# Attention and routed experts on one core: two banks for the turned weights, and a new order inside a step

## The chip, the cores and the metric

The kernel runs on one core of a Trainium2 chip. The metric is device time in microseconds, the median of several executions. Before the change it is 627.34 us (three executions, 626.08 to 628.61).

## The reference

The program computes attention with a window of 32 positions (heads 0 to 3) or with a window of 128 of which every fourth counts (heads 4 to 7), and sends the result, token by token, through one of eight experts. Cut to what matters:

```
B, H, S, D = 8, 8, 576, 64
scores = q @ k.T / sqrt(D), masked per head (rel < 32, or rel < 128 and rel % 4 == 0)
attn   = softmax(scores);  x = (attn @ v), laid out as (4608, 512)
logits = x @ w_gate                      # (4608, 8)
e      = argmax(logits, axis=1);  gate = softmax(logits)[e]
out    = gate * (relu(x @ w1[e]) @ w2[e])   # w1: 8 x 512 x 1024, w2: 8 x 1024 x 512
```

## The kernel before

The attention is worked off in 36 blocks of 128 rows, nine for each of the four batch pairs. One call of `step(n)` works on several blocks at once: it makes the scores of block n, turns the weights of block n - 1, multiplies by the values for block n - 2, turns the finished rows of block n - 3 and makes the routing logits of block n - 4. Steps 0 to 34 (`MEND = 35`) stand in a section in which TensorE, VectorE, ScalarE and SyncE issue strictly in the order in which the code names their work; the steps after that are put in order by the scheduler. After the attention come the experts, with TensorE busy nearly throughout.

The stages that the change touches, with their lines:

- `st_scores` (L290): 32 products of 64 x 64 tiles into the tiles `s` (one bank for each half g of the heads), after `st_mask` (L274) has written the mask there, one step earlier. A half's bank is free when `st_sub` has read it.
- `st_max` (L301) and `st_sub` (L306), VectorE: the maximum of a half, and the scores less the maximum into `d`. `d` is one tile for both halves and has one buffer.
- `st_exp` (L316), ScalarE: the exponential from `d` into `p`. `p` is one tile for both halves and has one buffer too.
- `st_trans` (L322), TensorE: four transposes of one half of `p` into the PSUM tile `pt`, tag `T`, one bank. `st_ptcopy` (L327), ScalarE: copies `pt` into `pts` (two buffers), and with that frees the bank.
- `st_av` (L337), TensorE: 32 products of `pts` with the values into `o` (one buffer of two banks). VectorE reads `o` in `st_z` (L347), `st_rz` (L352) and `st_x` (L357), which makes the rows `xs` and frees `o`.
- `st_xt` (L389), TensorE: four transposes of the rows into `tp`; `st_xcopy` (L397), ScalarE, copies them out.
- `st_logits` (L405), TensorE, in every third step (6, 9, 12 and so on): eight products into `ps_l`, tag `L`, one bank. `st_keep` (L418, L428), ScalarE, copies them out at the end of the step.
- Routing: after every ninth block `turn` (L485) transposes logits, first six tiles and one step later three. Groups 0 and 2 go to the bank with tag `E`, group 1 goes to tag `L`. VectorE reads them (L490). Other routing work of VectorE is drawn from a list by `pull_off` and `pull_spaced`, at fixed places of the step.
- `first.turn_x`, `first.high_x`, `first.low_x` (L806, L809, L813): in the two steps 35 and 36 the rows of the first expert's tokens are transposed and split into a high and a low part.
- In steps 9 to 13 ScalarE also makes the high halves of early expert weights (`high`, L742), at the end of a step.

PSUM has eight banks here: `X` one, `S0` and `S1` one each, `T` one, `O` two, `L` one, `E` one.

Of the kernel before, what the change touches and what calls it, by code (L numbers as in the profile page):

```python
# [9 lines left out]
F32 = mybir.dt.float32  # L10
# [17 lines left out]
P = 128  # L28
# [3 lines left out]
HP = H // 2  # L32
# [127 lines left out]
def attention_moe_kernel(ctx, tc, qk, v, wg, w, cst, tok, end, slots, mask, zero, out):  # L160
# [32 lines left out]
    psa = att.enter_context(tc.tile_pool(name="psa", bufs=1, space=PSUM))  # L193
# [17 lines left out]
    def load_qk(n):  # L211
        if n < total:
            nc.sync.dma_start(qkr[:, n % NRQ], qk[n])

    def load_v(n):
        if n < total:
            nc.sync.dma_start(vr[:, n % NRV], v[n])
# [98 lines left out]
        nc.scalar.activation(st["p", n][:, g], st["d", n][:, g], AF.Exp, scale=0.125)  # L316

    def st_trans(n, g):
        pt = psa.tile([P, HP, P], F32, tag="T", name="pt")
        st["pt", n] = pt  # L320
        for h in range(HP):
            nc.tensor.transpose(pt[:KB, h], st["p", n][:, g, h], ident)  # L322
# [69 lines left out]
    NG = 3  # L392
# [6 lines left out]
    def st_logits(n):  # L399
        if n % NG < NG - 1:  # L400
            return
        xt = st.pop(("xt", n // NG))
        ps_l = psa.tile([P, NG, P], F32, tag="L", name="ps_l")
        for c in range(4):
            nc.tensor.matmul(  # L405
                ps_l[32 * c : 32 * (c + 1)], lhsT=wgz[:, c], rhs=xt[:, c], start=True, stop=True
            )
        st["l", n] = ps_l
# [43 lines left out]
    def pull_pe(late=False):  # L452
        if side and side[0][0] == (2 if late else 1) and (
            ticks[0] - ticks[1] >= GAP or now[0] >= FREE
        ):
            side.pop(0)[1]()

    def pull_spaced():
        if slow:
            slow.pop(0)()  # L460

    def pull_off():
        ticks[0] += 1
        if side and not side[0][0]:
            ticks[1] = ticks[0]
            side.pop(0)[1]()

    def route(m, then=None, after=None):
# [7 lines left out]
        def turn(k):  # L476
            for k in k:
                if k % 2:
                    tl = psa.tile([P, NG, P], F32, tag="L", name="tl")
                else:  # L480
                    tl = pse.tile([P, NG, P], F32, tag="E", name="tl")
                    taken[0] = True
                for i in range(NG):
                    t = NG * k + i
                    nc.tensor.transpose(tl[:, i], lgs[:, t * P : (t + 1) * P], ident)  # L485
                box["tl", k] = tl
# [78 lines left out]
        def enter(ts):  # L565
# [3 lines left out]
            for t in ts:  # L569
                s1, b1 = hot.pop(t)  # L570
                nc.tensor.matmul(box["tb"], lhsT=s1, rhs=b1, start=t == 0, stop=t == NT - 1)

        on_pe(turn, (0, 1), late=True)
        off_pe(gather_parts, 0)
        off_pe(gather_parts, 1)
        on_pe(turn, (2,), late=True)
        off_pe(gather_parts, 2)
        off_both(
# [498 lines left out]
    first = statics[0]  # L1077
# [52 lines left out]
    def go(f, n):  # L1130
        if 0 <= n < total:
            f(n)

    def both(f, n, g):
        if 0 <= n < total:
            f(n, g)

    def step(n):
        now[0] = n
        if not turning or taken[0]:  # L1140
            pull_pe(late=True)
        go(st_scores, n)
        load_qk(n + 5)
        load_v(n + 3)
        turned = turning.pop(0) if turning and not taken[0] else None
        if turned is not None:
            first.turn_x(turned)
        both(st_trans, n - 1, 0)
        both(st_ptcopy, n - 1, 0)
        if turned is not None:  # L1150
            first.high_x(turned)
        both(st_max, n, 0)
        both(st_sub, n, 0)
        pull_spaced()
        go(st_av, n - 2)
        both(st_trans, n - 1, 1)
        both(st_ptcopy, n - 1, 1)
        both(st_exp, n, 0)
        both(st_max, n, 1)
        both(st_sub, n, 1)  # L1160
        go(st_xt, n - 3)
        go(st_xcopy, n - 3)
        both(st_exp, n, 1)
        if turned is not None:
            first.low_x(turned)
        else:
            pull_off()
        go(st_z, n - 2)
        go(st_rz, n - 2)
        pull_off()  # L1170
        go(st_x, n - 2)
        pull_spaced()
        go(st_xout, n - 2)
        pull_off()
        go(st_logits, n - 4)
        go(st_keep, n - 4)
        pull_pe(late=True)
        go(st_mask, n + 1)
        for _ in range(2):
            if spare:  # L1180
                high, low = spare.pop(0)
                high()
                low()
        pull_off()
        pull_pe()
        pull_off()
        for f in todo.pop(n, []):
            f()

    with tc.manual_schedule(engines=ENGS | {mybir.EngineType.SP}):  # L1190
        st_mask(0)
        for n in range(MEND):
            step(n)
    n = MEND
    while n < total + 5 or todo or spare:
        step(n)
        n += 1
# [367 lines left out]
```

## Time and profile before

| | |
|---|---|
| median of three executions | 627.34 us |
| the profiled execution, its own time | 627.71 us |
| its span, first to last instruction | 625.9 us |
[...]
| TensorE products busy | 601.3 us, 96% |
| VectorE busy, ScalarE busy | 340.5 us, 313.2 us |
| scores of step 3 to scores of step 35 start | 18.29 to 154.13 us |

In the rows below a line of the timeline gives start in us, duration in us, engine, line of the code, operation, tile written and tiles read, and how many instructions were merged. What stands in brackets is idle time of the engine just before, and who ended it. PE is the product, PEld the loading of its weights, DVE is VectorE, ACT is ScalarE, SPq is the queue of SyncE.

### The profile page before, as it was taken

The page shows a single profiled execution, that of the slowest core. Times are in us where ns is not written, and L with a number is a line of the kernel's source. Part 1 is how long each engine was busy: PE and PEld are TensorE (multiplying, and loading weights), DVE is VectorE, ACT ScalarE, POOL GpSimd, SP SyncE. Part 2 cuts the span into 40 slices and gives each one's busy share as a digit, 9 for nine tenths or more (in the row PEclk, how much of TensorE's full clock was granted, in tenths as well). Part 3 has the DMA queues.
Part 4 walks back from the last instruction along what each step waited for, and adds up shares of the span by engine and source line. Part 5 has one row for each costly group of instructions (what it writes and reads, how often), then busy time and mean ns, then how long its engine had stood idle before and what let it go on. Part 6 is the DMA issues. An engine that isn't in the chain of part 4 may idle for free. (4 is left out here: it accounts for less than half of the span.)

```text
span 625.9 us, 13313 instructions
## 1 busy us (share of the span) xinstructions
PE 601.3 (96%) x5299; PEld 490.4 (78%) x5299; DVE 340.5 (54%) x754; ACT 313.2 (50%) x606; POOL 249.3 (40%) x296
## 2 busy tenths in 40 slices
PE   7999999999989999999999999999999999999992
PEld 6877787788878888788888888888888888888771
DVE  3876787888593544563457255625643573453000
ACT  2668766676533541563456256535644563552110
POOL 0336666476826620451245125312522341253520
PEclk8999999999999999999999999999999999999997
DMA  8999999994237650573476267717743763476710
GB/s 319 411 384 414 413 403 410 396 331 139 66 99 230 208 185 29 181 257 117 151 241 231 84 221 240 241 55 236 259 162 112 243 234 119 172 241 252 276 49 21
DMA packets 43359, 138.17 MB, mean 221 GB/s; under 512 B 9008, under 2 KB 10416, under 8 KB 43248
## 3 DMA queue, kind: packets, MB, share of 16 engines
q1 hardware_dynamic: 23088, 78.30, 34.5%
q0 software_dynamic: 19776, 58.52, 27.0%
q8 instruction: 42, 0.69, 0.4%
q10 hardware_dynamic: 432, 0.49, 0.2%
q14 instruction: 21, 0.17, 0.1%
HBM read 117.65 MB, written 21.63 MB: 223 GB/s over the span
## 5 line engine op out<-in xcount | busy, mean ns | idle before, releaser
L731 DVE TENSOR_TENSOR wu<-raw,wu 128x512 fp32r<-128x512 f32 x200 | 128.7, 687 | 103.7 <-ACT wu L730 103.7
L877 PE MATMUL yps<-wu,h 128*128 128x512 f32 x696 | 170.5, 396 | 0.4 <-DVE wu L731 0.4
L846 PE MATMUL hps<-x,wu 128*128 128x512 f32 (+1 forms) x720 | 164.0, 385 | 0.2 <-DVE h L858 0.2
L846 PEld LDWEIGHTS hps<-x,wu 128*128 128x128 f32 x720 | 132.0, 188 | 27.6 <-DVE h L858 0.7
L877 PEld LDWEIGHTS yps<-wu,h 128*128 128x128 f32 x696 | 128.0, 188 | 27.4 <-DVE wu L731 0.8
L730 ACT CAST wu<-raw 128x512 fp32r<-128x512 f32 x200 | 113.3, 621 | 27.8 <-DMA raw<-in_w_dram,wi 17.2
L922 POOL DMA_INDIRECT raw<-in_w_dram,wi x40 | 39.4, 985 | 98.3 <-DVE wu L731 90.7
L858 DVE SCALAR_TENSOR_TENSOR h<-hps,h 128x512 fp32r<-128x512 f32 (+1 forms) x60 | 40.1, 670 | 47.8 <-ACT h L857 47.6
L327 ACT COPY pts<-pt 96x512 f32<-96x512 f32 x72 | 41.9, 582 | 46.7 <-PE pt L322 45.9
L767 POOL DMA_INDIRECT out_dram<-y,both_i x30 | 32.7, 1091 | 80.2 <-ACT y L766 60.1
L857 ACT ACTIVATE h<-hps 128x512 fp32r<-128x512 f32 (+1 forms) x60 | 34.8, 581 | 59.4 <-PE hps L846 52.3
L766 ACT ACTIVATE y<-yps,both_i 128x512 f32<-128x512 f32 x28 | 19.3, 688 | 68.5 <-PE yps L877 36.1
L301 DVE TENSOR_REDUCE nm<-s 128x4 f32<-128x384 f32 x72 | 39.5, 550 | 25.0 <-PE s L290 24.5
L322 PE MATMUL pt<-ident,p 128*96 128x128 f32 x288 | 47.3, 288 | 3.2 <-ACT pts L327 2.8
L337 PE MATMUL o<-vr,pts 96*64 96x65 f32 x1152 | 43.7, 227 | 2.0 <-issue 1.9
L337 PEld LDWEIGHTS o<-vr,pts 96*64 96x64 f32 x1152 | 38.1, 139 | 9.4 <-issue 8.4
L369 POOL DMA_DIRECT2D x_d<-xs x36 | 20.6, 572 | 60.9 <-DVE xs L357 26.3
L756 POOL DMA_INDIRECT xg<-x_d,both_i x30 | 32.2, 1074 | 29.5 <-PE tpx L806 11.5
L306 DVE TENSOR_TENSOR d<-s,nm 128x384 f32<-128x384 f32 x72 | 40.1, 557 | 4.6
L316 ACT ACTIVATE p<-d 128x384 f32<-128x384 f32 x72 | 37.6, 524 | 6.6 <-DVE d L306 6.6
L973 PE MATMUL ypd<-wu,hd 128*128 128x512 f32 x168 | 40.4, 391 | 0.0
L941 PE MATMUL hpd<-wu,xd 128*128 128x512 f32 x168 | 40.2, 393 | 0.0
(169 smaller groups left out, 680.7 us busy)
## 6 DMA issues: line engine op xcount, KB each, us to landing
raw<-in_w_dram SPq DMA_DIRECT2D x64, 512.0 KB, 4.3
qkr<-in_qk_dram SPq DMA_DIRECT2D x36, 576.0 KB, 8.3
vr<-in_v_dram SPq DMA_DIRECT2D x36, 520.0 KB, 8.8
x_d<-xs POOLq DMA_DIRECT2D x44, 128.0 KB
t_in<-tab SPq DMA_DIRECT2D x3, 320.0 KB
x_d<-xs POOLq DMA_DIRECT2D x8, 112.0 KB
x_d<-xs POOLq DMA_DIRECT2D x8, 96.0 KB
tab<-in_zero_dram SPq DMA_DIRECT2D x2, 320.0 KB
```

What stands on the lines that cost most here:

```text
L301: nc.vector.tensor_reduce(st["nm", n][:, g], st["s", n][g], axis=AX.X, op=ALU.max)
L306: nc.vector.tensor_tensor(st["d", n][:, g], st["s", n][g], st["nm", n][:, g].broadcast_to([P, HP, KB]), op=ALU.subtract,)
L322: nc.tensor.transpose(pt[:KB, h], st["p", n][:, g, h], ident)
L327: nc.scalar.copy(st["pts", n][:, g], st.pop(("pt", n))[:KB])
L337: nc.tensor.matmul(st["o", n][QB * j : QB * (j + 1), g, h], lhsT=pts[:, g, h, QB * j : QB * (j + 1)], rhs=vr[:KB, n % NRV, a : a + DH + 1] ...
L730: nc.scalar.copy(u[:, 0, sl], raw[:, sl])
L731: nc.vector.tensor_tensor(u[:, 1, sl], raw[:, sl], u[:, 0, sl].bitcast(F32), op=ALU.subtract)
L846: nc.tensor.matmul(hps[:, : self.ns], lhsT=u[:, wpart, fs], rhs=self.x[:, xpart, c, : self.ns], start=(k == 0), stop=(k == 11),)
L858: nc.vector.scalar_tensor_tensor(h[:, 1, :n], hps[:, :n], 0.0, h[:, 0, :n].bitcast(F32), op0=ALU.max, op1=ALU.subtract,)
L877: nc.tensor.matmul(yps, lhsT=self.h[f][:, hpart, ts], rhs=u[:, wpart, fs], start=f == 0 and k == 0, stop=f == 7 and k == 2,)
L941: nc.tensor.matmul(hps, lhsT=self.x[:, xpart, c], rhs=u[:, wpart, ns], start=(k == 0), stop=(k == 11),)
L973: nc.tensor.matmul(self.yps, lhsT=self.h[f // 4][:, hpart, f % 4], rhs=u[:, wpart, fs], start=f == 0 and k == 0, stop=f == 7 and k == 2,)
```

## The change

The tile `pt` gets two banks (tag `T`, `bufs=2`). The bank with tag `L` goes: the logits `ps_l` and the routing's group 1 (`tl`) are now taken from the same two banks `T`. The count of banks stays eight. Inside the step the order becomes: scores of block n, maximum and difference of its first half, values of block n - 2, the first expert's transposes where there are any, both halves of the turned weights of block n - 1, rows of block n - 3. The first exponential of block n is named between the first half's transposes and its copy, so on ScalarE it stands ahead of both copies of block n - 1, where it stood behind both. `first.high_x` moves from behind the first copy to behind the rows' transposes.

```
     def st_trans(n, g):
-        pt = psa.tile([P, HP, P], F32, tag="T", name="pt")
+        pt = psa.tile([P, HP, P], F32, tag="T", bufs=2, name="pt")
...
-        ps_l = psa.tile([P, NG, P], F32, tag="L", name="ps_l")
+        ps_l = psa.tile([P, NG, P], F32, tag="T", bufs=2, name="ps_l")
...
-                    tl = psa.tile([P, NG, P], F32, tag="L", name="tl")
+                    tl = psa.tile([P, NG, P], F32, tag="T", bufs=2, name="tl")
...
         turned = turning.pop(0) if turning and not taken[0] else None
+        both(st_max, n, 0)
+        both(st_sub, n, 0)
+        go(st_av, n - 2)
         if turned is not None:
             first.turn_x(turned)
         both(st_trans, n - 1, 0)
+        both(st_exp, n, 0)
         both(st_ptcopy, n - 1, 0)
-        if turned is not None:
-            first.high_x(turned)
-        both(st_max, n, 0)
-        both(st_sub, n, 0)
-        pull_spaced()
-        go(st_av, n - 2)
         both(st_trans, n - 1, 1)
         both(st_ptcopy, n - 1, 1)
-        both(st_exp, n, 0)
+        pull_spaced()
         both(st_max, n, 1)
         both(st_sub, n, 1)
         go(st_xt, n - 3)
+        if turned is not None:
+            first.high_x(turned)
         go(st_xcopy, n - 3)
         both(st_exp, n, 1)
```

## Rows read from the trace of the kernel before

**Rows 1.** The page, busy time, share and instructions of each engine.

```profile
PE 601.3 (96%) x5299; PEld 490.4 (78%) x5299; DVE 340.5 (54%) x754; ACT 313.2 (50%) x606; POOL 249.3 (40%) x296
```

**Rows 2.** Waits from 0 to 175 us: us in total, times, longest.

```profile
ACT pts L327 <- PE pt L322: 45.9, 48, 2.6
...
PEld pt L322 <- ACT pts L327: 4.7, 10, 1.3
...
PE pt L322 <- ACT pts L327: 2.8, 6, 1.2
```

**Rows 3.** Timeline of TensorE, step 8, to the scores of step 9.

```profile
37.77 0.83 PE L290 MATMUL s<-qkr 64*64 64x96 f32 x32
38.53 0.64 PE L322 MATMUL pt<-ident,p 128*96 128x128 f32 x4
39.10 1.15 PE L337 MATMUL o<-vr,pts 96*64 96x65 f32 x32
40.19 0.64 PE L322 MATMUL pt<-ident,p 128*96 128x128 f32 x4
40.66 0.60 PE L389 MATMUL tp<-ident,xs 128*128 128x128 f32 x4
41.20 0.36 PE L274 MATMUL s<-mk 64*64 64x384 bf16 x4
41.38 0.83 PE L290 MATMUL s<-qkr 64*64 64x96 f32 x32
```

**Rows 4.** Timeline of ScalarE, from the second copy of step 8 on.

```profile
40.87 0.58 ACT L327 COPY pts<-pt 96x512 f32<-96x512 f32 x1 [1.07 <-PE pt L322]
41.35 0.52 ACT L316 ACTIVATE p<-d 128x384 f32<-128x384 f32 x1
41.77 0.57 ACT L397 COPY xt<-tp 128x512 f32<-128x512 f32 x1
42.24 0.53 ACT L316 ACTIVATE p<-d 128x384 f32<-128x384 f32 x1
```

**Rows 5.** Timeline of VectorE, step 8, then the second half of step 17.

```profile
38.66 0.56 DVE L301 TENSOR_REDUCE nm<-s 128x4 f32<-128x384 f32 x1 [0.37 <-PE s L290]
39.33 0.56 DVE L306 TENSOR_TENSOR d<-s,nm 128x384 f32<-128x384 f32 x1
...
40.38 0.56 DVE L306 TENSOR_TENSOR d<-s,nm 128x384 f32<-128x384 f32 x1
...
41.28 0.69 DVE L357 TENSOR_TENSOR xs<-o,rz 128x512 f32<-128x512 f32 x1
...
81.62 0.56 DVE L306 TENSOR_TENSOR d<-s,nm 128x384 f32<-128x384 f32 x1
...
82.87 0.69 DVE L357 TENSOR_TENSOR xs<-o,rz 128x512 f32<-128x512 f32 x1
```

**Rows 6.** Timeline of TensorE, end of step 6: rows, logits, next mask.

```profile
32.59 0.60 PE L389 MATMUL tp<-ident,xs 128*128 128x128 f32 x4
33.12 0.85 PE L405 MATMUL ps_l<-xt,wgz 128*32 128x384 f32 x8
33.90 0.36 PE L274 MATMUL s<-mk 64*64 64x384 bf16 x4
```

**Rows 7.** Timeline, step 13: first copy, second turned half, routing's transposes.

```profile
63.13 0.58 ACT L327 COPY pts<-pt 96x512 f32<-96x512 f32 x1
...
63.77 0.64 PE L322 MATMUL pt<-ident,p 128*96 128x128 f32 x4 [1.17 <-ACT pts L327]
...
64.68 0.82 PE L485 MATMUL tl<-ident,lgs 128*128 128x128 f32 x6
```

**Rows 8.** Line 306 by itself: separate wait instructions in VectorE's queue, ns min/median/max.

```profile
L306 DVEq EVENT_SEMAPHORE  x32: 21/21/21, 11.0 to 156.7; - x32
```

**Rows 9.** Busy time from 160 to 200 us: length, then each engine.

```profile
160.00:200.00 40.00, 38.05 (x287) 31.18 (x282) 23.80 (x76) 16.50 (x36) 21.61 (x25) 1.00 0.44 136
```

**Rows 10.** Waits of SyncE's queue for TensorE, the values' loads.

```profile
SPq L217 <- PE o L337: 21.3, 16, 3.2
```

## The prediction

> **What bounds the kernel now.** I read the page first: TensorE's products are busy 96% of the span, VectorE 54%, ScalarE 50% [rows 1]. So whatever lengthens TensorE's sequence lengthens the kernel, and nothing else does until it makes TensorE wait. Then I read the waits of the attention: the one that the first edit aims at is TensorE waiting for the copy of turned weights, 2.8 us of idle products and 4.7 us of idle weight loads [rows 2]; the 45.9 us that ScalarE waits for TensorE are no loss by themselves. Then the timeline of one plain step, step 8. The reader should see that TensorE has no hole in it: scores to turned half 0.76 us, to values 0.57, to turned half 1.09, to rows 0.47, to the next mask 0.54, to the next scores 0.18, together 3.61 us [rows 3]. VectorE ends its second difference at 40.94, and the mask that needs it comes at 41.20 [rows 3, 5]; ScalarE idles 1.07 us ahead of the second copy [rows 4]. Both have a little air, and the question is whether the new order keeps it.
>
> In what follows S is the start of a step's scores and a the start of its values. A step ends when the mask for the next can be written.
>
> **TensorE's own sequence.** The new order is scores, values, half, half, rows, mask. Values to half 1.09, half to half 0.47 (as half to rows today), rows 0.47, mask 0.54, scores 0.18 are all in [rows 3]; only scores to values is new. Scores to a half takes 0.76 and cannot be less, since the 32 products themselves fill it. Going into the values costs 0.57 where a half to the rows costs 0.47, so 0.10 more for the entry. I take 0.76 + 0.10 = 0.86, since the values are entered here too: the plain step is then 0.86 + 1.09 + 0.47 + 0.47 + 0.54 + 0.18 = 3.61 us, unchanged. The bounds are 0.76 (no entry cost) and 0.95 (leaving the tiles of the scores costs as much again): over the 33 steps with values -3.3 to +3.0 us.
>
> [...]
>
> **The exponential ahead of the copies.** On ScalarE the order was copy, copy, exponential; it becomes exponential, copy, copy. `p` has one buffer, and the first exponential of block n writes the tile that both halves of block n - 1 are turned from. Does it wait for one half or for both? `d` is built alike, and there the trace tells: the first difference starts 0.67 us after its maximum, the separate wait instructions are 32 for 72 differences [rows 5, 8], so about one for each step and not one for each half. I take it that the buffer is given back whole. Then the second half, begun at a + 1.09 + 0.47, is with ScalarE 0.68 us later (40.19 to 40.87 [rows 3, 4]), and the exponential starts at a + 2.24. An exponential to the next instruction takes 0.42, a copy to the next 0.48 [rows 4]: the first copy starts at a + 2.66 and ends at a + 3.24, and TensorE sees it 0.06 later (63.13 + 0.58 to 63.77 [rows 7]), at a + 3.30. The second is done at a + 3.14 + 0.64 = a + 3.78. The next values come at a + 3.61 and need its half only after 16 of their 32 products, so they don't wait.
>
> **Logits without a bank of their own.** In every third step TensorE comes to the logits at a + 1.09 + 0.47 + 0.47 + 0.53 = a + 2.56 [rows 3, 6]. Both `T` banks then hold turned weights, and the first is free at a + 3.30. That is 0.74 us of waiting, with the mask and the next scores queued behind it on TensorE. Steps 6 to 36 have eleven logits that meet turned weights: +8.1 us. `st_keep` frees its bank well before the next step's second half, so it adds nothing.
>
> **The routing's group 1.** It comes 0.91 us after the second half's start plus half of the six transposes, 0.41 [rows 7], so at a + 1.56 + 0.91 + 0.41 = a + 2.88, and waits 0.42 for the same copy. Three routings in the ordered steps: +1.3 us.
>
> **The second exponential.** It starts after both copies and the rows' copy (0.48, 0.48, 0.47 [rows 4]) at a + 4.09 and is done at a + 4.68, which is S + 5.54, or 1.93 into the next step if this one was plain. There the first difference wants to start at 39.33 - 37.77 = 1.56 [rows 3, 5] and must wait for `d`: 0.37 late. The second difference then ends at 2.61 + 0.37 + 0.56, the mask may start 0.06 later, at 3.60, and TensorE comes to it at 3.43: a wait of 0.17 in a plain step that follows a plain one. After logits or routing the longer step hides it. Some five such steps are left: +0.9 us.
>
> **VectorE's rows.** The values now want `o` at S + 0.86, where they wanted it at S + 1.33. The rows of step 8 start at 41.28 and end at 41.97, 0.59 into the next step, so by themselves they pass. Where routing work stands before them (1.25 us after the second difference in step 17, against 0.90 [rows 5]) and the difference is late too, they miss by some tenths: 0 to 1 us in all, I take 0.5.
>
> **What the second bank gives.** The waits for the copy go, those of step 13 above all (1.17 us behind ScalarE's weight work [rows 7]): between 2.8 and 4.7 us [rows 2], I take 3.7.
>
> **Other moves, costed at nothing.** `pull_spaced` keeps its place on VectorE. The values free their slot earlier, so SyncE's loads, which wait 21.3 us for that [rows 10], go out up to half a microsecond earlier; no value load bounds a step. POOL's stores follow the rows, with slack as now. `high_x` comes behind both copies in steps 35 and 36, which makes the low part, and the bank `E` behind it, later: 0 to 2 us. After 160 us TensorE is idle 1.95 us of 40 [rows 9], and at most that much of a delay could vanish there. I set these two against each other.
>
> **Sum:** 8.1 + 1.3 + 0.9 + 0.5 - 3.7 = +7.1 us. The profiled execution, 627.71 us by itself (span 625.9), stands 0.37 above the median of 627.34, so the forecast is 634.5 us. About 0.5%, 3.1 us, is what a measurement of this kernel can tell from no change: 624.2 to 630.5.
>
> **The rivals.** (1) Not slower: halves are given back one by one. Then the exponential starts after the first half, at a + 1.09 + 0.68 = 1.77, the first copy is seen at a + 2.83, the logits wait 0.27 (3.0 us in all), group 1 not at all, and the second exponential is 0.47 earlier, so the difference is in time. 3.0 - 3.7 = -0.7, about 626.6 us. It decides when the exponential starts before the second half is turned. For it speaks that the values and transposes are followed by half; against it the count of wait instructions [rows 8]. (2) Only the gains: the logits find a bank at a + 2.56 and scores to values takes 0.76. 627.3 - 3.7 - 3.3 = 620.3 us. The copy would have to begin at a + 1.92, before the exponential that stands ahead of it; only another order on ScalarE than the code's allows that. (3) Scores to values takes 0.95, VectorE misses by its full 1 us and the late `high_x` costs 2 us: 634.5 + 3.0 + 0.5 + 2 = 640 us, and between here and there if part of it holds.
>
> **Chances.** The forecast, 631 to 637 us, 0.62; (3), 637 to 640, 0.20; (1) 0.11; (2) 0.07. The first two are slower, 0.82; (1) lies within 0.5%; (2) is faster. The two slower cases hold eight in ten, and with the lower bound of the sequence (-3.3) they reach from 630 to 640 us.
>
> **What would show it.** In the profile after: logits of each third step begin about 0.74 us after the place where the rows end, released by ScalarE's copy; the first exponential starts when the second half is turned, about S + 3.1, and copies follow it; scores to values is 0.86; TensorE's idle time ahead of a second turned half is gone. The prediction is wrong if the exponential starts near S + 2.6, if the logits follow the rows at once, or if scores to values is far from 0.86.

## The result and the profile after

| | before | after |
|---|---|---|
| median | 627.81 us (four executions, 626.08 to 628.61) | 635.74 us (four, 634.91 to 636.91) |
| profiled execution: time, span | 627.71 us, 625.9 us | 634.91 us, 633.1 us |
| scores of step 35 start | 154.13 us | 161.38 us |
| from there to the end of the span | 471.8 us | 471.7 us |

(One execution of the kernel before has come in since the forecast, which moved its median from 627.34 to 627.81.) The ratio is 1.0139 (95% interval 1.0115 to 1.0163): slower by less than 2%, but clear of the noise, by 7.9 us between the medians and 7.2 between the profiled executions. The forecast was 634.5 us with a range of 630 to 640. All of the loss lies before step 35; what comes after it takes as long as before and gives nothing back.

The page's busy times, for [rows 1]: every engine works as long as before, TensorE even 2.9 us less.

```profile
PE 598.4 (95%) x5299; PEld 492.2 (78%) x5299; DVE 339.6 (54%) x754; ACT 311.6 (49%) x606; POOL 250.1 (40%) x296
```

So the time went into waits. The waits of the first 185 us (us in total, times, longest), for [rows 2]:

```profile
ACT p L316 <- PE pt L322: 50.2, 32, 2.7
...
PEld ps_l L405 <- ACT pts L327: 8.0, 9, 0.9
...
PE ps_l L405 <- ACT pts L327: 5.8, 9, 0.6
...
DVE d L306 <- ACT p L316: 3.2, 8, 0.6
...
PE o L337 <- issue: 2.9, 3, 1.2
...
PE tl L485 <- ACT pts L327: 1.3, 3, 0.4
```

The line `pt` behind the copy, 2.8 us before [rows 2], is gone. In its place stand the logits and the routing's `tl` behind the same copy. A tenth wait of the logits, 0.69 us at 33.49 in step 6, stands under "issue" in this trace. On ScalarE it is the exponential that waits for TensorE, 32 times, where it was the copy.

TensorE in a plain step, step 7, for [rows 3]:

```profile
34.45 0.83 PE L290 MATMUL s<-qkr 64*64 64x96 f32 x32
35.22 1.15 PE L337 MATMUL o<-vr,pts 96*64 96x65 f32 x32
36.30 1.08 PE L322 MATMUL pt<-ident,p 128*96 128x128 f32 x8
37.22 0.60 PE L389 MATMUL tp<-ident,xs 128*128 128x128 f32 x4
37.75 0.36 PE L274 MATMUL s<-mk 64*64 64x384 bf16 x4
37.93 0.49 PE L290 MATMUL s<-qkr 64*64 64x96 f32 x11
```

Scores to scores is 3.48 us, where it was 3.61: here the new order is shorter. This step stands behind one with logits. A plain step behind a plain one has a wait, as step 11 from 52.63 to 56.33, 3.70 us. A longer wait of the same kind stands in step 18, here on TensorE and on VectorE:

```profile
84.44 0.93 PE L290 MATMUL s<-qkr 64*64 64x96 f32 x32
85.94 1.15 PE L337 MATMUL o<-vr,pts 96*64 96x65 f32 x32 [0.57 <-ACT xt L397]
```

```profile
85.00 0.69 DVE L357 TENSOR_TENSOR xs<-o,rz 128x512 f32<-128x512 f32 x1
```

The values come 1.50 us after the scores and not 0.76. The bracket names a copy, but the rows, which free `o`, end at 85.69, 0.25 us ahead of them. In the other steps with late values (but for step 27, where the scores themselves are slow, and those with a hole in the scores, below) the values also begin within 0.3 us of the rows' end, whatever the bracket names. So the values wait for the rows. Now step 12, which has logits, and step 13, which has the routing's transposes (for [rows 6] and [rows 7]):

```profile
59.96 1.08 PE L322 MATMUL pt<-ident,p 128*96 128x128 f32 x8
60.87 0.60 PE L389 MATMUL tp<-ident,xs 128*128 128x128 f32 x4
62.12 0.85 PE L405 MATMUL ps_l<-xt,wgz 128*32 128x384 f32 x8 [0.65 <-ACT pts L327]
62.90 0.36 PE L274 MATMUL s<-mk 64*64 64x384 bf16 x4
63.09 0.83 PE L290 MATMUL s<-qkr 64*64 64x96 f32 x32
63.85 1.16 PE L337 MATMUL o<-vr,pts 96*64 96x65 f32 x32
64.93 1.08 PE L322 MATMUL pt<-ident,p 128*96 128x128 f32 x8
65.85 0.60 PE L389 MATMUL tp<-ident,xs 128*128 128x128 f32 x4
66.29 0.49 PE L485 MATMUL tl<-ident,lgs 128*128 128x128 f32 x3
67.22 0.55 PE L485 MATMUL tl<-ident,lgs 128*128 128x128 f32 x3 [0.44 <-ACT pts L327]
```

And ScalarE beside it, for [rows 4]:

```profile
61.07 0.52 ACT L316 ACTIVATE p<-d 128x384 f32<-128x384 f32 x1 [1.86 <-PE pt L322]
61.50 1.05 ACT L327 COPY pts<-pt 96x512 f32<-96x512 f32 x2
62.45 0.59 ACT L397 COPY xt<-tp 128x512 f32<-128x512 f32 x1
```

Both lists are read together. The eight transposes end at 61.04; ScalarE, idle for 1.86 us, begins the exponential at 61.07, so it waited for the second half too. In all of the steps 4 to 34 the exponential begins at most 0.1 us after that half's end. Only behind it do the copies run, and the logits start at 62.12, one copy (0.58) after 61.50. Rows to logits is 1.25 us where it was 0.53 [rows 6]: 0.72 us lost.

### The profile page after: what moved, and what is told of

The parts are those of the page before. It is cut to its first block, busy times and chain, and to the rows that moved or that the text cites. A ratio compares the mean times of both kernels' runs of the same rounds, so it can differ in the third digit from the quotient of the medians.

```text
span 633.1 us, 13381 instructions
## 1 busy us (share of the span) xinstructions
PE 598.4 (95%) x5299; PEld 492.2 (78%) x5299; DVE 339.6 (54%) x754; ACT 311.6 (49%) x606; POOL 250.1 (40%) x296
## 5 line engine op out<-in xcount | busy, mean ns | idle before, releaser
L322 PE MATMUL pt<-ident,p 128*96 128x128 f32 x288 | 39.8, 282 | 0.0
L813 DVE TENSOR_TENSOR x<-tpx,x 128x512 fp32r<-128x512 f32 x30 | 20.7, 690 | 34.6 <-ACT x L809 34.6
```

## The experiments

**The exponential back behind the copies, all else of the change kept.**

```
         both(st_trans, n - 1, 0)
-        both(st_exp, n, 0)
         both(st_ptcopy, n - 1, 0)
         both(st_trans, n - 1, 1)
         both(st_ptcopy, n - 1, 1)
+        both(st_exp, n, 0)
         pull_spaced()
```

> The changed kernel with one line moved: the first exponential goes behind both copies on ScalarE, as before the change; banks and TensorE's order stay as changed. Theory A (the exponential that waits for the second turned half holds the copies, and the copies hold the bank that the logits need): the first copy starts 1.8 us after the start of the values instead of 2.7, logits and the routing's group 1 find a bank, the second difference is not late; a logits step falls from 4.98 to about 4.3 us, a plain one is 3.5, and the kernel ends 3 to 5 us below the kernel before, near 623 to 625 us. Theory B (the sharing of the two banks costs, whatever ScalarE's order): the waits stay, and it is near 634 us. Theory C (the values' earlier place costs, since rows and copies are not ready for them): waits of the values, not of the logits, and 628 us or more.

Measured: 626.61 us (624.53 to 628.8), ratio to the kernel before 0.9994 (0.998 to 1.0008). The whole loss is gone, so it hangs on the place of this one instruction. Rows to logits is 0.53 again in eight of the ten logits of steps 4 to 34 (the other two run at a granted TensorE clock of 0.5, one of them in part, below). But the gain of 3 to 5 us that was expected from the rest of the change is not there: on that the expectation missed.

**The kernel before, with the banks alone changed** (the three lines of `pt`, `ps_l` and `tl` from the diff; order as before).

> The kernel before with the banks of the change alone: turned weights, logits and the routing's group 1 share two banks, the order of the step stays. Theory A: at the old places the first copy is long done when the logits come, so no wait arises, and the waits of a turned half for a copy go; 2.5 to 4 us below the kernel before, near 624 us. Theory B: logits wait, 4 to 8 us above, 632 to 636 us.

Measured: 625.14 us (624.41 to 626.91), ratio 0.9979 (0.9965 to 0.9992), a gain of 1.6 us between the medians, where 2.5 to 4 were expected. Sharing two banks between turned weights, logits and routing costs nothing by itself: it needs the exponential ahead of the copies to cost something. The theory that the shared banks are the loss falls.

**Two buffers for `p`, the changed order kept.**

```
-            st["p", n] = ap.tile([P, 2, HP, KB], F32, name="p", bufs=1)
+            st["p", n] = ap.tile([P, 2, HP, KB], F32, name="p", bufs=2)
```

> The changed kernel with a second buffer for the exponentials p, nothing else. Theory A: the exponential no longer waits for the second turned half but only for its difference, about 0.9 us earlier; the copies follow, the logits find a bank but for about 0.1 us in some steps, and the kernel ends 3 to 4 us below the kernel before, near 624 us, though the order on ScalarE is the changed one. If it is the mere place of the exponential ahead of the copies that costs (it still waits for the difference), 630 us or more. Theory B: 634 us.

Measured: 625.98 us (625.4 to 627.17), ratio 0.9992 (0.9983 to 1.0002). The loss is gone here too, and the expected gain of 3 to 4 us is missing as in the first experiment; its trace has 5.1 us of the holes that are told of below. TensorE in its step 13, and ScalarE:

```profile
60.97 1.08 PE L322 MATMUL pt<-ident,p 128*96 128x128 f32 x8
61.88 0.60 PE L389 MATMUL tp<-ident,xs 128*128 128x128 f32 x4
62.32 1.06 PE L485 MATMUL tl<-ident,lgs 128*128 128x128 f32 x6
```

```profile
61.66 0.52 ACT L316 ACTIVATE p<-d 128x384 f32<-128x384 f32 x1
62.20 1.07 ACT L327 COPY pts<-pt 96x512 f32<-96x512 f32 x2
```

The exponential begins at 61.66, while TensorE is still turning the second half (60.97 to 62.05), and the routing's transposes run without a wait. So the place ahead of the copies alone does not bring the loss; what brings it is that the exponential waits there for the whole of a tile that has one buffer, with the copies queued behind it.

**Two buffers for `d`, the changed order kept.**

```
-            st["d", n] = ap.tile([P, 2, HP, KB], F32, name="d", bufs=1)
+            st["d", n] = ap.tile([P, 2, HP, KB], F32, name="d", bufs=2)
```

> The changed kernel with a second buffer for the differences d, nothing else. It takes away the wait of the first difference for the second exponential of the block before. Theory A: the waits of the logits stay, the plain steps that follow a plain one fall from about 3.7 to 3.8 to 3.5 us; 1 to 2.5 us below the changed kernel, near 634 us. If the late difference were the main cost, 629 us or less.

Measured: 635.28 us (634.4 to 636.09), ratio 1.0134 (1.0118 to 1.0151). That is 0.0005 below the changed kernel's ratio, within the intervals: a miss. The wait of `d` on the exponential, 3.2 us of VectorE's idle time in the changed kernel, is gone from the list of waits, yet the time stays. Step 11, a plain one behind a plain one, is 3.70 us long with either number of buffers: with two the first difference is in time, but the values still wait for the rows. This run also had a granted clock of 0.5 for 3.4 us after a hole of 1.47 us (below), so what the wait of `d` is worth in all isn't shown.

**Logits on a bank of their own.**

```
-        ps_l = psa.tile([P, NG, P], F32, tag="T", bufs=2, name="ps_l")
+        ps_l = pse.tile([P, NG, P], F32, tag="E", name="ps_l")
```

> The changed kernel with the logits in the bank of tag E instead of the two shared ones; group 1 of the routing stays in the shared ones, ScalarE's order stays as changed. It prices the wait of the logits by itself. Theory A, with the prediction's sum: the eleven waits of about 0.65 to 0.74 us go, the wait of group 1 (three times 0.4) and the late difference stay; 7 to 8 us below the changed kernel, 627 to 629 us. If the exponential's place costs mainly in other ways (values that wait for their copies), 631 us or more.

Measured: 629.61 us (627.76 to 630.63), ratio 1.0036 (1.0022 to 1.0051). TensorE, step 12:

```profile
58.46 0.60 PE L389 MATMUL tp<-ident,xs 128*128 128x128 f32 x4
58.99 0.85 PE L405 MATMUL ps_l<-xt,wgz 128*32 128x384 f32 x8
```

Rows to logits is 0.53 again. The ratio falls by 0.0103, which is 6.5 us of 627, a little less than the 7 to 8 expected: the logits' wait is most of the loss.

**Where the gain of the first experiment went.** Its profiled execution took 628.8 us, the longest of its twelve and 2.2 above their median, so what follows shows more loss than the median execution has. Its trace has holes in TensorE's work that nothing in the profile ends ("issue"). The largest:

```profile
42.29 0.94 PE L337 MATMUL o<-vr,pts 96*64 96x65 f32 x25
44.98 0.45 PE L337 MATMUL o<-vr,pts 96*64 96x65 f32 x7 [1.74 <-issue]
45.36 1.08 PE L322 MATMUL pt<-ident,p 128*96 128x128 f32 x8
46.27 1.01 PE L389 MATMUL tp<-ident,xs 128*128 128x128 f32 x4
47.22 1.51 PE L405 MATMUL ps_l<-xt,wgz 128*32 128x384 f32 x8
```

The hole stands between two products of one line, and the 4 transposes of the rows then take 1.01 us and the logits 1.51, where they took 0.60 and 0.85. The granted clock stands in a table of four stretches (length, busy time of PE, PEld, DVE, ACT, POOL, granted clock, DMA share, GB/s):

```profile
44.00:46.00 2.00, 1.02 (x13) 0.95 (x14) 1.09 (x5) 0.00 (x0) 0.08 (x1) 1.00 1.02 415
46.00:48.00 2.00, 2.00 (x17) 1.09 (x14) 0.59 (x1) 1.96 (x5) 1.10 (x3) 0.58 1.02 414
48.00:50.00 2.00, 2.00 (x44) 1.24 (x36) 0.00 (x0) 1.62 (x5) 0.50 (x2) 0.57 1.04 417
...
98.00:100.00 2.00, 2.00 (x13) 1.63 (x11) 0.67 (x2) 1.34 (x3) 1.46 (x3) 0.50 1.02 408
```

The granted clock falls to 0.5 from 46.31 to 49.73 us, after that idle stretch, and once more from 97.52 to 100.93, after a hole of 1.59 us; and the DMA engines are full (share 1.02 to 1.04 in the four stretches). The changed kernel's longest such hole is 1.19 us and the kernel's before 1.29, and their clock stays at 1.00 in the same stretch. A new theory: TensorE's instructions come late over the full DMA engines, and a denser order is hurt more. To test it, three kernels load q, k and v for the first blocks only.

```
-        if n < total:
+        if n < NRQ:
```

(in the loads of q and k and in those of v; the kernel before, the first experiment, the changed kernel). The experts get other counts of tokens there, so the total times say nothing; what is read is the stretch from the scores of step 4 to those of step 35.

> The kernel before, but queries, keys and values are loaded for the first six blocks alone and used over and over (the attention's results are those of other data, and the experts get other counts, so only the stretch from the scores of step 4 to those of step 35 is read: 132.0 us in the kernel before). Theory F (TensorE's unexplained holes are its instructions coming late over busy DMA rings, and a denser order of products makes them longer): the holes go, and the stretch is about 128 us. If the holes are something else, they stay and it is 131 to 133 us.

> The changed kernel with the exponential behind the copies, with loads for six blocks alone as in the run before it. With all loads the stretch from step 4 to step 35 is 134.1 us, 2 us longer than in the kernel before though its clean steps are 0.13 us shorter. Theory F: without the traffic the holes go and the stretch is 3 to 5 us shorter than that of the kernel before with few loads, about 124 us. If the loss lies in waits between the engines, it stays within 1 us of it.

> The changed kernel with loads for six blocks alone. With all loads the stretch from step 4 to step 35 is 140.2 us. It prices the waits between the engines without the holes: by the prediction's terms and the clean steps of the trace 5 to 7 us more than the kernel before with few loads, about 134 us.

The two ends of the stretch on TensorE, for the kernel before, the first experiment and the changed kernel, each with few loads:

```profile
20.63 1.00 PE L290 MATMUL s<-qkr 64*64 64x96 f32 x32
...
149.66 0.83 PE L290 MATMUL s<-qkr 64*64 64x96 f32 x32
```

```profile
21.35 0.87 PE L290 MATMUL s<-qkr 64*64 64x96 f32 x27
...
145.34 0.83 PE L290 MATMUL s<-qkr 64*64 64x96 f32 x32
```

```profile
21.05 1.00 PE L290 MATMUL s<-qkr 64*64 64x96 f32 x32
...
155.83 0.83 PE L290 MATMUL s<-qkr 64*64 64x96 f32 x32
```

| scores of step 4 to scores of step 35, us | all loads | few loads | price of the loads |
|---|---|---|---|
| kernel before | 132.02 | 129.03 | 3.0 |
| exponential behind the copies | 134.13 | 123.99 | 10.1 |
| changed kernel | 140.19 | 134.78 | 5.4 |

From 20 to 150 us the DMA engines were then busy 0.38 of the time and not 0.97 (the second kernel with few loads, and the changed kernel with all):

```profile
20.00:150.00 130.00, 126.82 (x2691) 107.27 (x2691) 112.28 (x321) 94.73 (x208) 81.08 (x123) 1.00 0.38 126
```

```profile
20.00:150.00 130.00, 115.64 (x2412) 96.10 (x2412) 97.73 (x267) 85.94 (x185) 70.55 (x106) 1.00 0.97 368
```

With few loads none of the three kernels has such a hole in this stretch. (The changed kernel has one line with "issue", 0.69 us ahead of the logits of step 6: the tenth wait of the logits, as above.) So the loads make the holes. In its profiled execution the order without the early exponential loses 10.1 us to the loads, 7.1 more than the kernel before: 4.8 us are the holes between products, and part of the rest is the 6.8 us at a granted clock of 0.5 behind two of them. The medians, 0.9994, say that nearly all of the gain of 5.0 is lost. How much the holes' sum varies from execution to execution isn't shown: there is one trace of each kernel.

The places of the holes speak for late delivery of instructions. Both pages have a queue whose kind is called instruction:

```profile
q8 instruction: 42, 0.69, 0.4%
```

That is 42 packets of 16 KB each. TensorE has 10,744 records (weight loads, products and its queue's own) in the kernel before and 10,779 in the changed one, so about 256 records a packet, an estimate that takes all 42 packets for TensorE's. With all loads, the seven traces (both kernels and the first five experiments) have 34 holes of over 0.1 us in this stretch, and when the records are numbered in order, every one ends at a number that leaves 193 or 194 when divided by 256. In the two kernels a packet lands 1.3 to 1.6 us before the end of each of their nine holes (43.47 for the end at 44.98 in the kernel before; 58.16 for 59.69 in the changed kernel). No experiment moved that queue by itself, so the late delivery is the author's estimate and not shown.

The three rows also take the change apart. Exponential ahead of the copies: 134.78 - 123.99 = +10.8 us. Everything else, without the loads' noise: 123.99 - 129.03 = -5.0. The loads cost 5.4 - 3.0 = 2.4 more than before in these two executions. Together +8.2, and 140.19 - 132.02 is 8.2.

## Why the prediction was right, step by step

- **The exponential waits for the whole of `p`.** Right, and shown by the second buffer for `p`, which takes the loss away. The count of separate waits [rows 8] had pointed the right way; rival (1) falls, since the exponential starts as the second half ends.
- **The logits' wait, 0.74 us in eleven steps, +8.1.** Right in place and size, but for one step: ten logits wait 0.72 us each (0.76 in step 6), 7.2 us; the eleventh, in step 36 behind the ordered section, follows its rows at once. Their own bank took 6.5 us off the whole kernel.
- **The routing's group 1, +1.3.** Three waits, 1.3 us of idle products; with few loads the steps 13, 22 and 31 are 2.0 us longer between rows and mask than in the kernel before.
- **The late second exponential, +0.9.** Right in cause, wrong in where it costs. The first difference waits for it 8 times, as in step 11, a plain step behind a plain one, whose scores start at 52.63: the difference starts 2.02 us behind them, where it wants 1.56, so 0.46 late for 0.37 forecast.

```profile
53.52 0.56 DVE L301 TENSOR_REDUCE nm<-s 128x4 f32<-128x384 f32 x1 [0.17 <-PE s L290]
54.65 0.56 DVE L306 TENSOR_TENSOR d<-s,nm 128x384 f32<-128x384 f32 x1 [0.58 <-ACT p L316]
```

  The forecast put the cost at the mask; with few loads it waits about 0.1 us in five steps, 0.5 in all, and more falls on the next term.
- **VectorE's rows, +0.5.** The term that was missed most. The forecast let the rows pass by themselves and let the next values not wait at all. With few loads, 11 of the 31 steps from 4 to 34 begin their values late behind the rows, 3.4 us more in all than in the kernel before; without the early exponential it is 1.8.
- **TensorE's own sequence, 0, from scores to values at 0.86.** Mis-sized: 0.76 (34.45 to 35.22), the lower bound, wherever the values do not wait. The change from the scores' tiles to the values' costs nothing beyond the 32 products, and a plain step without a wait is 3.48 us, 0.13 less than the 3.61 of [rows 3], which would be 4.3 us over 33 steps. The forecast had added an entry cost seen only behind a transpose. With few loads the rows start 2.76 us behind the scores where they started 2.89, 4.2 us over 31 steps.
- **The second bank, -3.7.** Right, though the run with the banks alone is only 1.6 us faster. In the kernel before, the second half begins late behind the copy in 13 of the 31 steps, 4.0 us in all, not counting steps with a hole (3.5 with few loads). That lies between the idle products, 2.8, and the idle weight loads, 4.7, as the forecast took it. With the banks alone it begins late only in the five steps with a hole; those are late by 4.2 us, where the holes of the kernel before make 2.6. What the banks alone give with few loads wasn't run.
- **Not foreseen: the holes.** The holes and the loads' other delays cost the changed kernel 2.4 us more than the kernel before. Nothing in the forecast stood for them.

The terms side by side. All but the loads are read from the two traces with few loads, the kernel before and the changed one:

| term, us | forecast | measured, step 4 to step 35 |
|---|---|---|
| logits' wait | +8.1 | +7.2 |
| group 1 | +1.3 | +2.0 |
| mask behind the late difference | +0.9 | +0.5 |
| values that wait for the rows | +0.5 | +3.4 |
| TensorE's sequence | 0 | -4.2 |
| second bank | -3.7 | -3.5 |
| routing's products in step 26 | 0 | +0.3 |
| loads (one execution each) | 0 | +2.4 |
| together (unrounded) | +7.1 | +8.2 |

So the two mechanisms that the forecast rested on hold: the exponential waits for the whole of `p`, and the logits wait behind it. That the sum came so near, +7.1 against +7.2 in the profiled executions, is in part luck: two terms were wrong by 3 to 4 us, the values' wait and the sequence, and they nearly cancel; the holes were not in it. The kernel ends only 7.2 later and not 8.2 because step 4 begins 0.9 us earlier than before (21.19 for 22.12), which the forecast hadn't set; of the time before it TensorE spent 6.8 us at a granted clock of 0.5 in the kernel before and 3.4 in the changed one. The order without the early exponential does not beat the kernel before; the banks alone do, at 0.9979.

## What to carry to other kernels

Before an instruction is named earlier on an engine that works in order, ask which buffer it overwrites, when the last reader of the whole tile is done, and what stands behind it: here one exponential held up a copy, the copy a bank, and the bank TensorE, for 10.8 us. Sharing banks between stages cost nothing here (ratio 0.9979) while the copy that frees them ran at once, and that should be tried apart from any new order. A gain in a stage in which the DMA engines are full, as here at a share of 0.97, is not counted until a run shows it: the denser order kept almost none of its 5 us there.

## What the hardware showed that was not expected

- TensorE stood still for up to 1.74 us between two products of one line without a wait that the profile shows, in a stretch in which the DMA engines were full (share 0.97 from 20 to 150 us in the two kernels; at a share of 0.37 to 0.38 not once). Counted in groups of 256 records, about as many as come on a packet by the estimate above, all 34 such holes end at number 193 or 194.
- After the holes of 1.47, 1.59, 1.71 and 1.74 us the granted clock was 0.5 for 3.4 us each, as from 46.31 to 49.73 in the first experiment. After the others in that stretch, the longest of 1.29 us, it stayed at 1.00.
- Products of 64 x 64 tiles straight into the values' products cost no time of their own where they did not wait (0.76 us, as into a transpose), while the values behind a transpose started 0.57 after it against 0.47 for the rows [rows 3].
